# Sliding-window attention and a two-layer product: turning q and k by crossbar DMA, and storing 128 rows in one or two DMAs

## The chip, the cores and the metric

One core of one Trainium2 chip. The metric is device time in microseconds (us), the median of several executions; lower is better. Executions of one kernel mostly agree within about 1%; a run over 1.5% above the fastest of its kernel counts as slow. Ratios use the fast runs alone; medians and ranges below are of all runs. Inputs and output are float32; the kernel computes in float16 with float32 sums.

## The reference

Eight batches of 8-head attention over 576 positions (head size 64), where each position sees itself and the 127 before it, with a bias linear in the distance. The result goes token by token through two matrices with an ELU between.

```python
scores = scale * np.matmul(q, k.transpose(0, 1, 3, 2)) + bias      # bias = -slope * |distance|
attn   = softmax(where((rel >= 0) & (rel < 128), scores, -1e9))
x      = np.matmul(attn, v).transpose(0, 2, 1, 3).reshape(8 * 576, 512)
h      = x @ w_in                                                  # 512 -> 2048
g      = np.where(h > 0, h, np.exp(np.minimum(h, 0)) - 1)
out    = g @ w_out                                                 # 2048 -> 512
```

## The kernel before

One program in steps, 16 to a batch. Each step does one bank of attention scores (`sp`) and values (`av`) of the current batch, and, some steps behind, one tile of the hidden product (`hp`, 128x512) with its ELU, and four matmuls of the output (`op`). All engines run in the order in which the program lists their work, and so does SP's DMA queue. Four parts of it matter here.

q and k arrive with 4 positions per partition (`stq`). TensorE transposes ("turns") them, in four groups of eight transposes a batch, and ScalarE and VectorE copy them out of PSUM into `QK`, which keeps positions in blocks of 32 with the same remainder modulo 4:

```python
def transposes(b, hp):
    t = ps_s.tile([128, 2, 2, 4, 2, 32], F16, name="tp", tag="sps")
    ...                                        # eight nc.tensor.transpose(t[...], stq[b][...], ident)
    for odd in range(2):
        ...
        if hp % 2: nc.scalar.copy(o, i)
        else:      V.tensor_copy(o, i)
```

A finished block of attention, 128 tokens (`xn`), is turned for the hidden product. From batch 2 on (`XBAR = 2`) a crossbar DMA does it, which transposes 16-bit data while it moves them, from SP's queue:

```python
def turn(b, i):
    if b >= XBAR:
        nc.sync.dma_start_transpose(out=xT[:, :, o:o + n], in_=x[0:n, :])
        return
    ...                                        # batches 0 and 1: four TensorE transposes and a copy
```

From batch 3 on v is loaded through SP's queue too, four DMAs for 128 positions (q and k come through GpSimd's own queue). GpSimd casts v to float16, in line with the `min` that it does for each ELU:

```python
nc.sync.dma_start(t[32 * j:32 * j + 32, :, :], v[b, :, 128 * n + j:128 * n + 128:4, :]...)   # load_v
nc.gpsimd.tensor_scalar(out=VP[...], in0=vf.pop((b, n))..., ...)                                 # cast_v
nc.gpsimd.tensor_scalar(out=e, in0=e, scalar1=1.0, scalar2=0.0, op0=ALU.min, op1=ALU.max)        # hidden
```

The tokens run in blocks of 32 with the same remainder modulo 4, so a tile of 128 output rows goes back in up to four stores of 32 rows, each with a DRAM step of four rows:

```python
r.append((c - c0, out[b * S + 128 * n + p // 32:b * S + 128 * n + 128:4, :]))    # rows_of
...
for p0, rows in rows_of(512 * t + 128 * ts):
    nc.sync.dma_start(rows, ob[p0:p0 + rows.shape[0], :])                        # output
```

The softmax here doesn't subtract the row's maximum and nothing guards it: scores larger than these inputs give would overflow.

## Time and profile before

| before | value |
|---|---|
| time | 367.06 us (366.23 to 367.32, three runs) |
| span of the profiled run, clock granted to TensorE | 363.7 us, 0.995 |
| SP's queue: stores, v loads, crossbar transposes | 128 + 8 larger, 85, 30 |
| a crossbar transpose of 128x512: time in SP's queue | 1.2 us |

In the lines of the profile PE is TensorE, PEld its weight loads, DVE VectorE, ACT ScalarE, POOL GpSimd, and SPq SP's DMA queue; L451 is line 451 of the kernel.

### The profile page before, as it was taken

To read this page: it belongs to the slowest core of one execution; us is meant where nothing else is said; L and a number is where in the kernel's file an instruction comes from. 1 tells how busy PE (TensorE), PEld (TensorE's weight loads), DVE (VectorE), ACT (ScalarE), POOL (GpSimd) and SP (SyncE) were. 2 spreads that over 40 slices of the span, in tenths; PEclk is the share of its full clock that TensorE was granted. 3 is DMA by queue.
4 is the path that set the end of the run, shared out by engine and by line. 5 is a ranking of instruction groups with operands and counts; after the bars stand their busy time and mean duration, and the time that the engine had idled before them with its cause. 6 is when DMAs were issued, how large, how long until landed. Compare 5 with 4: busy or idle time off the path is not lost.

```text
span 363.7 us, 9613 instructions
## 1 busy us (share of the span) xinstructions
PE 340.3 (94%) x3790; PEld 251.6 (69%) x3790; DVE 243.5 (67%) x574; ACT 206.7 (57%) x349; POOL 145.7 (40%) x229
## 2 busy tenths in 40 slices
PE   6878997999979999989999999999999999999994
PEld 6766775777647667767777777777777777666651
DVE  6479889678886776666676767776776756634430
ACT  4355583666537655765566665666567565543431
POOL 9146623434314723472346334642433232233320
PEclk9899999999999999999999999999999999999999
DMA  8999999839243973497448934793631222211113
GB/s 114 198 206 119 228 107 183 151 80 155 38 103 89 133 108 84 110 128 110 98 94 127 127 88 100 120 136 82 102 84 45 52 47 45 51 43 47 29 43 73
DMA packets 81948, 37.06 MB, mean 102 GB/s; under 512 B 51952, under 2 KB 77296, under 8 KB 81904
## 3 DMA queue, kind: packets, MB, share of 16 engines
q0 software_dynamic: 34064, 15.40, 35.5%
q1 hardware_dynamic: 47840, 21.06, 25.6%
q8 instruction: 29, 0.48, 0.6%
q14 instruction: 15, 0.12, 0.1%
HBM read 36.70 MB, written 9.44 MB: 127 GB/s over the span
## 4 chain that ended last, share of the span: by engine, by line
PE 65%; DVE 14%; ACT 9%; DMA 7%; issue 3%; POOL 1%; SPq 0%; ACTq 0%; POOLq 0%
PE hp L451 27%; PE op L492 25%; PE sp L348 5%; ACT QK L322 5%; DVE VP L116 4%; DMA vs<-in_v_dram 3%; PE av L394 3%; DVE g L463 3%; ACT EX L372 2%; DVE QK L324 2%; ACT e L455 2%; DVE EX L380 2%; DMA xT<-xn 2%; DMA stq<-in_q_dram 1%; DVE xn L415 1%
## 5 line engine op out<-in xcount | busy, mean ns | idle before, releaser
L456 POOL TENSOR_SCALAR e<-e 128x512 f32<-128x512 f32 x144 | 88.6, 615 | 199.9 <-ACT e L455 199.9
L451 PE MATMUL hp<-xT,wi 128*128 128x256 f16 (+3 forms) x1536 | 150.3, 246 | 8.1 <-DVE g L463 3.6
L451 PEld LDWEIGHTS <-wi 128*128 128x128 f16 x1536 | 121.5, 98 | 49.9 <-DVE g L463 5.5
L455 ACT ACTIVATE e<-hp 128x512 f32<-128x512 f32 x144 | 86.0, 597 | 119.0 <-PE hp L451 110.0
L492 PE MATMUL op<-wo,g 128*128 128x512 f16 x576 | 146.4, 379 | 0.0
L463 DVE SCALAR_TENSOR_TENSOR g<-e,hp 128x512 f16<-128x512 f32 x144 | 98.0, 681 | 23.9 <-POOL e L456 22.7
L380 DVE TENSOR_TENSOR EX<-EX,band 128x512 f16<-128x512 f16 x112 | 49.8, 445 | 57.1 <-ACT EX L372 57.0
L372 ACT ACTIVATE EX<-sp 128x512 f16<-128x512 f32 x128 | 75.9, 593 | 13.3 <-PE sp L368 8.6
L492 PEld LDWEIGHTS <-g 128*128 128x128 f16 x576 | 51.2, 98 | 36.9
L348 PE MATMUL sp<-QK 128*128 128x128 f16 (+3 forms) x576 | 49.8, 213 | 0.0
L394 PE MATMUL av<-VP,EX 128*128 128x65 f16 x576 | 38.6, 193 | 4.3 <-DVE EX L380 2.7
L394 PEld LDWEIGHTS <-EX 128*128 128x128 f16 x576 | 31.6, 98 | 8.7 <-DVE EX L380 4.2
L415 DVE TENSOR_TENSOR xn<-av,rden 128x256 f16<-128x256 f32 x80 | 34.0, 424 | 2.8
L348 PEld LDWEIGHTS <-QK 128*128 128x128 f16 (+1 forms) x576 | 31.3, 97 | 1.0 <-issue 0.2
L496 ACT COPY ob<-op 128x512 f32<-128x512 f32 x36 | 21.1, 586 | 14.3 <-PE op L492 6.4
L322 ACT COPY QK<-tp 64x1024 f16<-64x1024 f16 x28 | 28.1, 1005 | 1.6 <-PE tp L312 1.4
L414 DVE RECIPROCAL rden<-av 128x4 f32<-128x4 f32 x80 | 14.4, 180 | 16.0 <-PE av L394 14.6
L134 POOL TENSOR_SCALAR VP<-vf 128x512 f16<-128x512 f32 (+1 forms) x25 | 19.5, 779 | 2.7 <-DMA vf<-in_v_dram 2.7
L324 DVE COPY QK<-tp 64x1024 f16<-64x1024 f16 x28 | 19.2, 684 | 1.1 <-PE tp L312 0.8
L312 PE MATMUL tp<-ident,stq 128*128 128x128 f16 x224 | 17.1, 219 | 2.3 <-ACT QK L322 1.0
L312 PEld LDWEIGHTS <-stq 128*128 128x128 f16 x224 | 13.8, 98 | 3.4 <-issue 3.2
L116 DVE COPY VP<-vs 32x512 f16<-32x512 f16 x48 | 14.9, 310 | 1.3 <-DMA vs<-in_v_dram 0.5
(70 smaller groups left out, 118.5 us busy)
## 6 DMA issues: line engine op xcount, KB each, us to landing
out_dram<-ob SPq DMA_DIRECT2D x128, 64.0 KB, 1.7
vf<-in_v_dram SPq DMA_DIRECT2D x80, 64.0 KB, 2.3
stq<-in_k_dram POOLq DMA_DIRECT2D x7, 512.0 KB, 6.4
stq<-in_q_dram POOLq DMA_DIRECT2D x7, 512.0 KB, 7.5
wi<-in_moe_w_in_dram POOLq DMA_DIRECT2D x4, 512.0 KB, 13.8
wo<-in_moe_w_out_dram POOLq DMA_DIRECT2D x4, 512.0 KB, 15.1
QK<-TQ SPq DMA_DIRECT2D x2, 576.0 KB, 8.0
vs<-in_v_dram POOLq DMA_DIRECT2D x2, 512.0 KB, 9.9
```

The lines of the kernel that those rows point to most:

```text
L312: nc.tensor.transpose(t[:, g, w, :, j, :], stq[b][:, w, 2 * hp + g, 2 * j:2 * j + 2, :].rearrange("p a d -> p (a d)"), ident)
L322: nc.scalar.copy(o, i)
L348: nc.tensor.matmul(t[:, o:o + n], qk[0:r, h, 1, kc:kc + 128], qk[0:r, h, 0, qc:qc + n], start=b > 0 or o == 0, stop=b > 0)
L372: nc.scalar.activation(e[:, 0:512], t, AF.Exp, scale=0.125)
L380: V.tensor_tensor(out=e, in0=e, in1=band[:, c:c + n].unsqueeze(1).broadcast_to([128, 512 // n, n]), op=ALU.min)
L394: nc.tensor.matmul(a[:, l, :], e[:, c:c + 128], vp[:, n, h, 0:D + 1], start=st, stop=sp)
L415: V.tensor_tensor(out=xnt[b, i][:, 4 * half:4 * half + 4, :], in0=a[:, :, 0:D], in1=r.unsqueeze(2).broadcast_to([128, 4, D]), op=ALU.mult)
L451: nc.tensor.matmul(p[:, l * w + u0:l * w + u1], w_in_sb[:, c, fc * 128:(fc + 1) * 128], xT[:, c, x0:x0 + u1 - u0], start=(c == 0), stop=(c ...
L455: nc.scalar.activation(e, p, AF.Exp)
L456: nc.gpsimd.tensor_scalar(out=e, in0=e, scalar1=1.0, scalar2=0.0, op0=ALU.min, op1=ALU.max)
L463: V.scalar_tensor_tensor(out=gs[t][:, f0:f0 + nf, c0:c0 + w], in0=sh(es.pop((t, j))), scalar=1.0, in1=sh(hps.pop((t, j))), op0=ALU.subtrac ...
L492: nc.tensor.matmul(ops[t], gs[t][:, fc, ts * 128:(ts + 1) * 128], w_out_sb[:, fc, :], start=(fc == 0), stop=(fc == NFC - 1))
```

## The change

Its intent: TensorE is the bound, so take the transposes of q and k of batches 2 to 7 off it (and their copies off ScalarE). The crossbar turns them, in eight DMAs a batch, and VectorE puts the result in block order, within SBUF. To make room in SP's queue, a store's rows are reordered by the DRAM side of its pattern, so that one or two DMAs do what up to four did. And the copies that place v of batch 2 move some steps earlier. The core of the diff, with cuts marked:

```diff
+        def cross(b, n):
+            w, hp = 1 - n // NP, n % NP
+            ...
+            nc.sync.dma_start_transpose(
+                out=tq[b][:, w, 2 * hp:2 * hp + 2, :, :].rearrange("p h a c -> p (h a) c"),
+                in_=stq[b][:, w, 2 * hp:2 * hp + 2, :, :].rearrange("p h j d -> p (h j d)"))
+
+        def uncross(b, n):
+            w, j = 1 - n // 4, n % 4
+            r = slice(64 * (j % 2), 64 * (j % 2) + 64)
+            V.tensor_copy(
+                QK[b % 2][0:64, :, w, 0:512].rearrange("p h (n j i) -> p h n j i", j=4, i=32)[:, :, :, j, :],
+                tq[b][r, w, :, j // 2, :].rearrange("p h (n i) -> p h n i", i=32))
...
+                n, p = divmod(o, 128)
+                k = min(128 - p, S - o, c0 + 128 - c)
+                if n < 4:
+                    rows = out[b * S + 128 * n:b * S + 128 * n + 128, :].rearrange(
+                        "(i j) d -> j i d", j=4)[p // 32:(p + k) // 32, :, :]
...
-                for hp in range(NP):
-                    at(s0 + ((5, 9, 10, 13) if b > 1 else (9, 10, 13, 14) if b else (14, 14, 15, 15))[hp],
-                       transposes, b + 1, hp)
+                if b == 0:
+                    for hp in range(NP):
+                        at((14, 14, 15, 15)[hp], transposes, b + 1, hp)
+                else:
+                    for n in range(8):
+                        at(s0 + (n if b > 1 else 6 + n // 2), cross, b + 1, n)
+                        at(s0 + (5 + n if b > 1 else 12 + n // 2), uncross, b + 1, n)
...
-        at(33, load_v4_tail, 2)
+        at(22, load_v4_tail, 2)
...
-            at(32 + n, place_v4, 2, n)
+            at(24 + 2 * n, place_v4, 2, n)
```

More of the change, by code (lines that the diff above doesn't have):

```diff
@@ L71 @@
     xT = one([128, 4, RING], F16, "xT")
-    stq, stt, vf, vs = {}, {}, {}, {}
+    stq, stt, vf, vs, tq = {}, {}, {}, {}, {}
     def load_qk(b, w, h0=0, h1=H):
@@ L324, in transposes @@
                     V.tensor_copy(o, i)
+        def cross(b, n):
+            w, hp = 1 - n // NP, n % NP
+            if n == 0:
+                tq[b] = stage.tile([128, 2, H, 2, 128], F16, name="tq", tag="tq", bufs=1)
+            nc.sync.dma_start_transpose(
[7 more added lines that the diff above has]
+                tq[b][r, w, :, j // 2, :].rearrange("p h (n i) -> p h n i", i=32))
         def transposes_tail(b):
@@ L472, in rows_of @@
                 b, o = divmod(c, S)
-                if o < 512:
-                    n, p = divmod(o, 128)
-                    r.append((c - c0, out[b * S + 128 * n + p // 32:b * S + 128 * n + 128:4, :]))
-                    c += 32
-                else:
-                    r.append((c - c0, out[c:c + 64, :]))
-                    c += 64
+                n, p = divmod(o, 128)
[3 more added lines that the diff above has]
+                        "(i j) d -> j i d", j=4)[p // 32:(p + k) // 32, :, :]
+                else:
+                    rows = out[c:c + k, :]
+                r.append((c - c0, c - c0 + k, rows))
+                c += k
             return r
@@ L496, in output @@
                 nc.scalar.copy(ob, ops[t])
-                for p0, rows in rows_of(512 * t + 128 * ts):
-                    nc.sync.dma_start(rows, ob[p0:p0 + rows.shape[0], :])
+                for p0, p1, rows in rows_of(512 * t + 128 * ts):
+                    nc.sync.dma_start(rows, ob[p0:p1, :])
         spare = ps_o.tile([128, DO], F32, name="spare", tag="op")
```

## The prediction

> **What bounds the kernel now.** I read the page's busy shares first, then the chain of work that ended last (its summary, then its pieces in order of time over one batch), then the groups of instructions for the durations of what goes, then the DMA issues and the DMA queue's timeline, because the change moves work there.
>
> The page: busy time, share of the span, and the chain's summary.
>
> ```profile
> PE 340.3 (94%) x3790; PEld 251.6 (69%) x3790; DVE 243.5 (67%) x574; ACT 206.7 (57%) x349; POOL 145.7 (40%) x229
> ...
> PE 65%; DVE 14%; ACT 9%; DMA 7%; issue 3%; POOL 1%; SPq 0%; ACTq 0%; POOLq 0%
> ```
>
> TensorE is nearly always busy and makes 65% of the chain. So removing TensorE work pays, as long as nothing else ends up in the chain. The chain in order of time shows a step of the schedule without transposes and the place where the transposes of q and k cut in:
>
> ```profile
> 205.54 0.87 PE hp L451 x8
> 206.41 0.24 PE av L394 x8
> 206.66 0.22 PE sp L348 x4
> 206.88 0.86 PE op L492 x4
> ...
> 216.08 0.87 PE hp L451 x8
> 216.95 0.12 PE av L394 x4
> 217.07 0.22 PE sp L348 x4
> 217.30 0.45 PE tp L312 x8
> 217.74 0.86 PE op L492 x4
> ```
>
> From 205.54 to 216.08 are five steps, 2.11 us each: 0.87 + 0.12 + 0.22 + 0.86 and a little more where a block begins. A group of eight transposes adds 0.45. Where ScalarE copies the result out of PSUM the chain leaves TensorE altogether:
>
> ```profile
> 199.90 1.00 ACT QK L322
> 200.90 0.01 issue
> 200.91 1.02 ACT QK L322
> 201.93 0.04 issue
> 201.97 0.39 PE tpt L330 x8
> 202.36 0.97 PE op L492 x4
> ```
>
> The same piece comes back at 239.13 and 275.90, so a batch of 16 steps takes 36.77 us. Sixteen steps at 2.11 are 33.7, with the tail's transposes (0.39, they stay) 34.1. So the transposes of q and k cost about 2.65 us a batch: 4 x 0.45 = 1.8 of TensorE, the rest waits on the copies.
>
> The groups that go, and the DMA queue's timeline of one batch start (both of before):
>
> ```profile
> L322 ACT COPY QK<-tp 64x1024 f16<-64x1024 f16 x28 | 28.1, 1005 | 1.6 <-PE tp L312 1.4
> L324 DVE COPY QK<-tp 64x1024 f16<-64x1024 f16 x28 | 19.2, 684 | 1.1 <-PE tp L312 0.8
> ```
> ```profile
> 203.98 1.73 SPq L498 DMA_DIRECT2D out_dram<-ob  x4
> 205.82 2.72 SPq L423 DMA_TRANSPOSE xT<-xn  x2
> 208.63 2.01 SPq L126 DMA_DIRECT2D vf<-in_v_dram  x4
> 212.56 2.14 SPq L498 DMA_DIRECT2D out_dram<-ob  x4
> 214.80 1.19 SPq L423 DMA_TRANSPOSE xT<-xn  x1
> 216.09 4.45 SPq L126 DMA_DIRECT2D vf<-in_v_dram  x8
> ```
>
> A crossbar transpose of 128x512 holds SP's queue for about 1.2 us (1.3 with the gap after it), a v load about 0.5, a store about 0.43. SP's queue is in order, and is free about a third of this stretch.
>
> **What the Trainium skill says.** (1) "DMA: Bandwidth & Descriptors", section "Why a DMA increments its semaphore by 16 and not by 1": a DMA runs on the largest k up to 16 that divides the slowest dimension of both access patterns, on the lowest-numbered engines. The new stores have a DRAM pattern of 4x32x512 or 2x32x512, so k would be 4 or 2 in place of 16. No run of before has such a DMA, so its trace cannot confirm it. (2) Same page, "Latency and other measured facts": a DMA transpose moves 261 GB/s; for 128 KB an estimate of 0.5 us. The trace agrees: its packet records show 32 packets of 256 B on each engine at 15 to 18 ns, 0.5 to 0.6 us, with 2.4 us from issue to landing. The crossbar itself is cheap; the issue is not. (3) "VectorE: DVE Perf Modes", "Why PSUM operands drop a tier" and the tier table before it: a copy from PSUM gets at most 2x, a 16-bit copy within SBUF 4x. The trace agrees: from PSUM 1024 elements take 684 ns and 512 take 417 (0.52 ns each); within SBUF 512 take 285 and 256 take 210 (0.29 each).
>
> **The change part by part.**
> *TensorE:* batches 2 to 7 lose 24 groups of 8 transposes, 24 x 0.45 = 10.8 us. *ScalarE* loses 24 copies of 1.005, 24 us. *VectorE* loses 24 x 0.684 = 16.4 us and gets 48 copies of 64x1024 within SBUF, estimated at 285 + 512 x 0.29 = 0.43 us each, 20.6 in all: 4 us more. It is at about 1.6 us a step, so per step (cut 0.445, elu 0.68, normalize 0.38 on average, reorder 0.43) it comes to about 2.0 with the gaps, just under TensorE's 2.11.
> *SP's queue* gets 48 transposes (48 x 1.3 = 62 us) and loses some 80 of 136 stores (about 35 us).
>
> *Batches 2 to 6 running* (they turn 3 to 7): 5 x 2.65 = 13.2 us gained at most.
>
> *Batch 1 running* (it turns batch 2): there the profile shows VectorE as the limit, the copies that place v in steps 32 to 35 (five steps from 92.27 to 107.62, 3.07 each). They move into steps 24 to 30, but the new reorders of batch 2 and both tails lie there too. VectorE over steps 24 to 31: 8 x 1.73 + 5.1 (place) + 3.7 (reorder) + 1.7 (tails) = 24.4 us against 19.1 that these steps took; steps 32 to 36 then take 5 x 2.11 = 10.6 in place of 15.3. Sum 35.0 against 34.4: nothing gained, within 2 us.
>
> *Waits for the new transposes.* I walked SP's queue over a batch start in the order of the built program, with the times above: the fourth transpose of k starts about 10 us after step 0 and lands at 11.5, when VectorE wants it at about 13; the last of q starts about 20.2 and lands 22.6, when VectorE wants it at 21.5. So VectorE waits about 1 us for q; the slack before TensorE feels it is 0.5 to 1 us (elu must end before the hidden product two steps on). After a pair of 2x32x512 stores the transposes queue on two engines behind 64 packets of 2,048 B. Such packets took 84 to 167 ns in before, median 122; with few engines writing I take the low end, 85 to 90, so 64 are 5.6 us, and then the waits are 2 to 3 us. Mean: 0.8 us a batch, 4 us in all.
>
> *A turned block that is needed soon.* Blocks of batches 2 and 3 are turned three steps before use; in before one landed late (5.5 us at 158.3, TensorE idle 1.1). Behind a pair of stores, at step 46, I expect about 2 us of new waiting.
>
> *The end.* Before, the last output copy starts at 359.1 and the last store's packets end near 362.4. The last four tiles have seven stores of 2x32x512 and one plain one. On two engines a tile needs 64 x 85 ns = 5.4 us, while TensorE finishes one every 3.45: from 347.1 they end at 352.5, 358.6, 364.0, and the last (32 packets and four of the plain store) at 367.1. That is 4.7 us later.
>
> Sum: 367.1 - 13.2 + 0.6 + 4 + 2 + 4.7 = 365.2; I lower it to 364.5, as the ScalarE time freed shortens some waits on its exps.
>
> **Rivals.** *A: the stores spread over all 16 engines after all* (if the pattern is cut otherwise). Then the end is 0.4 us shorter, the pair waits go: 367.1 - 13.2 - 0.4 + 2 = 355 to 357. For it: the stores of before with 32 or 64 rows land in 1.7 us and someone tuned this kernel. Against: the rule of (1) and the built program's pattern. One in five. *B: SP's queue becomes the bound.* For it: 27 us of issue in a batch of 34, two thirds in the first nine steps; v loads come late, so GpSimd's casts, which stand in order with its mins, hold up elu. Against: the walk above keeps up but for 1 us. It would eat all of the 13 and, with the end, give 370 to 376. One in five. *C: two-engine stores run at the median 122 ns*, 7.8 us a tile: the end grows by 12 us in place of 4.7, total 372. *D: VectorE's reorders, which read SBUF in a fast mode, slow GpSimd's mins.* The skill's "SBUF — State Buffer", section "SBUF: two separate sides", calls their port pair an exclusive lock. The mins take 615 ns, and 48 x 0.43 could be added at worst, mostly hidden since GpSimd is busy 40%: under 2 us.
>
> **Range and chances.** Step gains are read off the trace and are firm (13 us, give or take 1). What I am unsure of takes them back: the end 0 to 12, waits 0 to 12. From 356 (all but the gain small) to 374 (B or C). Faster by over 2% means under 359.7: rival A and half of the good cases of the waits, 0.30. Slower than 374.4 needs B and C together or a stall that I do not see: 0.14. Between: 0.56.
>
> **What would show it.** Right: batches 2 to 6 repeat every 34 to 36 us; no ScalarE copies of QK in the chain but for batches 0 and 1; waits of VectorE's reorder for the DMA tq<-stq of about 1 us each batch; the stores' time to landing up from 1.7 to 4 us or more; the last store landing 5 us or more after the last output copy. Wrong: stores that still land in 2 us (A); SP never waiting for a sender in the first half of a batch and VectorE or GpSimd waiting 3 us and more for DMA (B); the reorder at 0.7 us in place of 0.43.

## More of the kernel before

Start with the view of waits. A line says which engine and instruction waited, for whom, the total in us, how often, and the longest wait. Three lines of before:

```profile
PEld L451 <- DVE g L463: 5.5, 5, 1.4
...
PE hp L451 <- DVE g L463: 3.6, 6, 0.9
...
POOL VP L134 <- DMA vf<-in_v_dram: 2.7, 1, 2.7
```

TensorE hardly waits for VectorE's ELU (`g`), and GpSimd waits once for a v load. The lines on the clock and the DMA engines, in 40 equal slices of the span, in tenths:

```profile
PEclk9899999999999999999999999999999999999999
DMA  8999999839243973497448934793631222211113
```

TensorE keeps its full clock from the third slice on, and the DMA engines are about half idle after the first fifth.

## The result, and the profile after

**430.0 us** (median; 427.02 to 433.81, four runs, the last of which counts as slow) against 367.07 (366.23 to 367.32, four runs): 17% slower. The ratio is 1.169, with a 95% interval of 1.163 to 1.176. Ratios here are the mean time of one kernel's fast runs over the mean of the other's of the same rounds, so not quite the ratio of the medians quoted beside them.

The page after, the lines that answer to those of before:

```profile
PE 353.5 (83%) x3598; PEld 255.1 (60%) x3598; DVE 252.0 (59%) x598; ACT 184.9 (43%) x325; POOL 144.2 (34%) x229
...
PEclk9978999968997879869979998799996999999996
DMA  9999999992779986598898999699984435411111
...
PE 52%; DMA 25%; DVE 10%; SPq 5%; issue 2%; ACT 2%; POOL 1%; DVEq 0%; ACTq 0%; POOLq 0%
PE hp L467 23%; PE op L510 19%; DMA tq<-stq 12%; DMA xT<-xn 9%; PE sp L364 5%; PE av L410 3%; DMA vs<-in_v_dram 3%; DVE g L479 3%; DVE VP L116 2%; SPq L331 2%; SPq L439 2%; DMA stq<-in_q_dram 1%; ACT EX L388 1%; DVE EX L396 1%; DVE QK L338 1%
```

TensorE's share fell from 94% to 83%, and the chain now holds 25% of DMA and 5% of SP's queue (`SPq`): the new transposes (`tq<-stq`) 12%, the old ones (`xT<-xn`) 9%. ScalarE's copies of QK are gone from the chain, as intended. But TensorE has 192 matmuls fewer and yet is busy for 13 us longer, and its granted clock falls in many slices (mean 0.915 in place of 0.995). The waits:

```profile
DVE QK L338 <- DMA tq<-stq: 51.2, 12, 8.5
...
PE hp L467 <- DVE g L479: 41.0, 12, 7.8
...
POOL VP L134 <- DMA vf<-in_v_dram: 15.1, 7, 5.5
...
PE hp L467 <- DMA xT<-xn: 8.2, 4, 4.7
```

VectorE's reorder waits for the crossbar 51 us in all, twelve times. As VectorE is in order too, the ELU behind the reorder comes late, and TensorE waits 41 us for it: the same waits seen one engine further on. The groups:

```profile
L467 PE MATMUL hp<-xT,wi 128*128 128x256 f16 (+3 forms) x1536 | 163.6, 259 | 54.5 <-DVE g L479 41.0
...
L338 DVE COPY QK<-tq 64x1024 f16<-64x1024 f16 x48 | 23.7, 494 | 51.8 <-DMA tq<-stq 51.2
```

Now SP's queue at a batch start (start, time held, what, how many), to be laid beside the stretch of before in the prediction, and three pieces of the chain from the same stretch:

```profile
290.17 1.24 SPq L439 DMA_TRANSPOSE xT<-xn  x1
291.50 1.52 SPq L331 DMA_TRANSPOSE tq<-stq  x1
293.11 2.12 SPq L439 DMA_TRANSPOSE xT<-xn  x1
295.28 1.26 SPq L331 DMA_TRANSPOSE tq<-stq  x1
296.63 2.01 SPq L126 DMA_DIRECT2D vf<-in_v_dram  x4
298.69 1.21 SPq L331 DMA_TRANSPOSE tq<-stq  x1
300.00 0.57 SPq L516 DMA_DIRECT2D out_dram<-ob  x1
300.69 2.14 SPq L439 DMA_TRANSPOSE xT<-xn  x1
302.88 1.74 SPq L331 DMA_TRANSPOSE tq<-stq  x1
...
315.44 1.97 SPq L331 DMA_TRANSPOSE tq<-stq  x1
```
```profile
302.88 5.30 DMA tq<-stq
...
315.44 6.18 DMA tq<-stq
322.77 1.87 PE hp L467 x8
```

The queue has no gap in this stretch. The fourth crossbar transpose of q and k starts 12.7 us after the first line, the eighth 25.3 us after it, and they land 5.3 and 6.2 us after their start (the pieces of the chain run to the landing). The last piece is what follows on TensorE, at half rate. The timeline shows an earlier stall and a shorter one (start, duration, the idle time before and who ended it):

```profile
267.63 0.42 DVE L338 COPY QK<-tq 64x1024 f16<-64x1024 f16 x1 [8.54 <-DMA tq<-stq]
...
268.70 1.86 PE L467 MATMUL hp<-xT,wi 128*128 128x256 f16 x8 [7.81 <-DVE g L479]
...
309.36 1.03 PE L467 MATMUL hp<-xT,wi 128*128 128x256 f16 x8 [3.60 <-DVE g L479]
```

VectorE waits 8.54 us for the crossbar, TensorE 7.81 us for VectorE, and then runs at half rate. The Trainium skill's "TensorE: Matmul & The Clock Gate", section "What's actually happening", says that the clock falls to half after an idle window of about 3.4 us and returns after about as long a busy one. The trace agrees: eight matmuls take 1.03 to 1.04 us in this view when nothing has been amiss, still 1.03 after 3.60 us of idling, and 1.86 to 1.87 after 4.89, 5.38 and 7.81 us. (The border isn't sharp: in the run with merged transposes below 3.39 us of idling were enough.) The next ones are slow too (four of `op` at 271.00: 1.91 us in place of 1.03), so a long wait costs its own length and some 2 us more.

Where is the time lost? Each batch has one spot that is easy to find, VectorE's copy of the tail's transposes in step 14 (`QK<-tpt`). Its start in each batch, from the timelines:

| start of that copy in batch, us | 1 | 2 | 3 | 4 | 5 | 6 | end of span |
|---|---|---|---|---|---|---|---|
| before | 89.2 | 129.1 | 166.4 | 203.4 | 240.2 | 277.0 | 363.7 |
| after | 98.6 | 151.4 | 198.7 | 242.9 | 288.7 | 334.2 | 427.9 |
| later by | 9.4 | 22.3 | 32.2 | 39.5 | 48.5 | 57.2 | 64.2 |

Every batch that turns q and k by crossbar loses 7 to 13 us, and the end another 7. (Of batch 1's 9.4 us, 2.6 were lost by step 25 of the program, 1.7 of them at the start.)

### The profile page after: what moved, and what is told of

Same layout as the page of the kernel before. It is cut to its first block, busy times and chain, and to the rows that moved or that the text cites. A ratio compares the mean times of both kernels' runs of the same rounds, so it can differ in the third digit from the quotient of the medians.

```text
span 427.9 us, 9192 instructions
## 1 busy us (share of the span) xinstructions
PE 353.5 (83%) x3598; PEld 255.1 (60%) x3598; DVE 252.0 (59%) x598; ACT 184.9 (43%) x325; POOL 144.2 (34%) x229
## 4 chain that ended last, share of the span: by engine, by line
PE 52%; DMA 25%; DVE 10%; SPq 5%; issue 2%; ACT 2%; POOL 1%; DVEq 0%; ACTq 0%; POOLq 0%
PE hp L467 23%; PE op L510 19%; DMA tq<-stq 12%; DMA xT<-xn 9%; PE sp L364 5%; PE av L410 3%; DMA vs<-in_v_dram 3%; DVE g L479 3%; DVE VP L116 2%; SPq L331 2%; SPq L439 2%; DMA stq<-in_q_dram 1%; ACT EX L388 1%; DVE EX L396 1%; DVE QK L338 1%
## 5 line engine op out<-in xcount | busy, mean ns | idle before, releaser
L467 PE MATMUL hp<-xT,wi 128*128 128x256 f16 (+3 forms) x1536 | 163.6, 259 | 54.5 <-DVE g L479 41.0
L467 PEld LDWEIGHTS <-wi 128*128 128x128 f16 x1536 | 130.4, 104 | 102.7 <-issue 57.5
L510 PE MATMUL op<-wo,g 128*128 128x512 f16 x576 | 153.7, 394 | 0.0
L338 DVE COPY QK<-tq 64x1024 f16<-64x1024 f16 x48 | 23.7, 494 | 51.8 <-DMA tq<-stq 51.2
L364 PE MATMUL sp<-QK 128*128 128x128 f16 (+3 forms) x576 | 52.1, 220 | 0.9 <-DVE QK L338 0.5
L410 PE MATMUL av<-VP,EX 128*128 128x65 f16 x576 | 40.3, 198 | 4.2 <-DVE EX L396 2.5
L364 PEld LDWEIGHTS <-QK 128*128 128x128 f16 (+1 forms) x576 | 33.0, 101 | 2.1 <-issue 0.6
L430 DVE RECIPROCAL rden<-av 128x4 f32<-128x4 f32 x80 | 14.2, 178 | 22.1 <-PE av L410 21.1
L523 PE MATMUL spare<-ident 128*128 128x128 f16 x94 | 9.0, 272 | 1.6 <-DVE ident L175 1.6
L523 PEld LDWEIGHTS <-ident 128*128 128x128 f16 x94 | 8.1, 126 | 1.7 <-DVE ident L175 1.6
L352 DVE COPY QK<-tpt 64x512 f16<-64x512 f16 x16 | 6.7, 418 | 0.2
## 6 DMA issues: line engine op xcount, KB each, us to landing
wi<-in_moe_w_in_dram POOLq DMA_DIRECT2D x4, 512.0 KB, 10.8
```

Of the source, the lines that this page charges most:

```text
L338: V.tensor_copy(QK[b % 2][0:64, :, w, 0:512].rearrange("p h (n j i) -> p h n j i", j=4, i=32)[:, :, :, j, :], tq[b][r, w, :, j // 2, :].re ...
L364: nc.tensor.matmul(t[:, o:o + n], qk[0:r, h, 1, kc:kc + 128], qk[0:r, h, 0, qc:qc + n], start=b > 0 or o == 0, stop=b > 0)
L410: nc.tensor.matmul(a[:, l, :], e[:, c:c + 128], vp[:, n, h, 0:D + 1], start=st, stop=sp)
L467: nc.tensor.matmul(p[:, l * w + u0:l * w + u1], w_in_sb[:, c, fc * 128:(fc + 1) * 128], xT[:, c, x0:x0 + u1 - u0], start=(c == 0), stop=(c ...
L510: nc.tensor.matmul(ops[t], gs[t][:, fc, ts * 128:(ts + 1) * 128], w_out_sb[:, fc, :], start=(fc == 0), stop=(fc == NFC - 1))
```

## The experiments

Theory at the outset (S): the stores that run on few DMA engines hold the transposes up. Rival (T): SP's queue has too much to issue, whatever the stores. The runs were made in four lots, each beside runs of the kernel before (367.6 to 368.6 us, median of the lot). Fourteen kernels ran, all with correct results.

**First the rule on which theory S rests**: how many engines does a store use? In the packet records of SP's queue each DMA closes with 4-byte packets, one for each engine that it uses, a transpose with 32. Before: 226 plain DMAs of 16 and 30 transposes of 32 make 4,576; counted: 4,576. After: 78 transposes x 32 + 98 plain ones x 16 + 16 stores (4x32x512) x 4 + 32 stores (2x32x512) x 2 = 4,192; counted: 4,192. (The same sums come out in the runs with merged transposes, 4,960, and with the new stores and no transpose, 1,696.) So the new stores do run on four and two engines, as the prediction took from the skill. Its rival A is out.

**Old stores, the rest of the change** (one part undone).

```diff
-                for p0, p1, rows in rows_of(512 * t + 128 * ts):      # and rows_of as before
-                    nc.sync.dma_start(rows, ob[p0:p1, :])
+                for p0, rows in rows_of(512 * t + 128 * ts):
+                    nc.sync.dma_start(rows, ob[p0:p0 + rows.shape[0], :])
```

> The changed kernel with the stores of before (four DMAs of 32 rows, each over 16 engines), all else as changed. Theory S (the few-engine stores are the cause: 64 packets on each of two or four engines stand ahead of every later DMA of SP's queue, and a transpose that waits on one engine holds its packets open on all): 355 to 365 us, tq and xT landing in 2.5 to 4 us again, no packets of over 2 us. Theory T (48 more crossbar transposes are too much, whatever the stores: SP's issue, or transposes holding each other up): 410 us or more, VectorE still waiting some 40 us for tq.

Measured: 410.76 us, ratio 1.117 (1.110 to 1.123). So the transposes alone cost 42 us and the stores 19 of the 63. Its profile: slow (416.99 us, clock 0.937), so I take from it only what the waits are for:

```profile
DVE QK L338 <- DMA tq<-stq: 55.1, 12, 10.7
PE hp L467 <- DVE g L479: 53.7, 16, 10.1
```

The crossbar's data land within a median of 2.7 us of their issue here, yet VectorE waits as long as in the changed kernel. So few-engine stores aren't needed for the waits, and the time is in T's range. Late issue isn't all of it, though: in the two longest waits of this run (10.7 and 9.5 us) VectorE had waited for 3.6 and 2.7 us when the transpose was issued, which then took 7.0 and 6.8 us to land. The run with unread transposes, a fast one, shows what they met.

**The new stores alone, in the kernel before** (the reverse edit in the other kernel).

> The kernel before with the new stores alone (two or four engines). Theory S: its 30 transposes of xn get caught too, and the end is 6 us longer: 373 to 385 us, with packets of some us around the turns. Theory T: the end alone, 371 to 374 us.

Measured: 388.19 us, ratio 1.051 (1.044 to 1.059): the stores cost 20 us without any new transpose, more than either theory said. The chain and SP's queue at the worst place:

```profile
210.41 15.86 DMA xT<-xn
```
```profile
209.17 1.13 SPq L500 DMA_DIRECT2D out_dram<-ob  x2
210.41 4.06 SPq L423 DMA_TRANSPOSE xT<-xn  x1
```

A crossbar transpose behind a pair of two-engine stores holds the queue for 4.06 us in place of 1.2 and lands 15.9 us after its start. (Loads of k and q by GpSimd's queue, issued at 208.26 and 212.98, run in this stretch too.) The waits for turned blocks:

```profile
PE hp L451 <- DMA xT<-xn: 10.3, 3, 4.3
PEld L451 <- DMA xT<-xn: 9.0, 2, 4.8
```

By the copy of step 14, batches 1 to 6 are 2.8, 6.7, 13.7, 14.9, 16.7 and 16.7 us later than before. The first 2.8 us are there in step 12 of batch 0 already, before any store, so they aren't the stores'. The loss comes mostly in batches 2 and 3 (their blocks are turned three steps before use) and then at the end (24 us later there).

**Rows reordered on chip, so that a store of 64 rows uses 16 engines** (the changed kernel with fewer stores that spread).

```diff
-                            p[:, l * w + u0:l * w + u1], w_in_sb[:, c, fc * 128:(fc + 1) * 128],
-                            xT[:, c, x0:x0 + u1 - u0], ...)
+                            p[:, l * w + u0:l * w + u1].rearrange("p (g i j) -> p g j i", i=32, j=2),
+                            w_in_sb[:, c, fc * 128:(fc + 1) * 128],
+                            xT[:, c, x0:x0 + u1 - u0].rearrange("p (g j i) -> p g j i", i=32, j=2), ...)
...
+                        "(i j) d -> i j d", j=4)[:, p // 32:p // 32 + 2, :]        # the store's DRAM side
```

> The changed kernel, with rows put in order when the hidden product is written to PSUM, so that each 64 rows are one store whose DRAM pattern is 32x2x512, which divides over 16 engines: as few stores as changed, but on all engines. Theory S: 353 to 363 us, a little under e1 since SP issues 72 stores and not 136. Theory T: 410 or more. If the strided PSUM write slows TensorE, hp matmuls get longer than 258 ns at full clock.

Measured: 466.0 us, ratio 1.269, a miss, though useful. Hidden matmuls that write PSUM with a step of two elements take 364 ns each in place of 246 to 259 (TensorE 96% busy, clock 0.996). VectorE waits for the crossbar only 4.3 us here: with steps that long, SP's queue keeps up. The edit adds a cost of its own, so it can't be read as a trial of the stores.

**Stores issued by ScalarE** (old stores; `nc.sync.dma_start` becomes `nc.scalar.dma_start` for them).

> As e1, but the 16-engine stores are issued by ScalarE's queue, so SP's queue has 136 issues less. Theory S: 352 to 363 us; if SP's issue was what made transposes late, faster than e1 by 3 us or more, else the same. Theory T by SP's issue: well under 430, 380 to 400. Theory T by transposes holding each other: 410 or more.

Measured: 416.36 us, ratio 1.131 (1.123 to 1.138); its profile is slow. The waits for the crossbar fall to 5.2 us, as they should if SP's queue was too full, but ScalarE, in order like the others, now carries the stores' issue (10% of the chain) and waits that the profile puts down to stores (28.6 us before its exps). One in-order queue is relieved, another loaded. By its time alone the run fell to the branch "transposes holding each other" (410 or more); the short waits for the crossbar speak against that reading, but ScalarE's load keeps the run from deciding.

**The reorders three steps later** (old stores), to see if slack is all that is missing.

```diff
-                        at(s0 + (5 + n if b > 1 else 12 + n // 2), uncross, b + 1, n)
+                        at(s0 + (8 + n if b > 1 else 12 + n // 2), uncross, b + 1, n)
```

> As e1 (changed kernel, 16-engine stores of before), but VectorE's reorders for batches 3 to 7 stand three steps later (steps 8 to 15 of the batch before, not 5 to 12). Theory Q (SP's in-order queue falls behind its schedule, VectorE stands at the reorder until the transpose lands, TensorE then idles and comes back at half clock): the waits go, 360 to 372 us, VectorE's wait for tq under 12 us in place of 55. Theory R (transposes are slow in themselves or slow other DMAs, whenever they are used): 395 us or more.

Measured: 405.53 us, ratio 1.102 (1.095 to 1.110): a miss, and by its time on the side of theory R. The waits:

```profile
POOL VP L134 <- DMA vf<-in_v_dram: 49.5, 11, 8.6
...
DVE QK L338 <- DMA tq<-stq: 15.9, 5, 4.4
```

VectorE's waits fall from 55 to 16 us, and GpSimd's waits for v rise from 7 to 50. The v loads stand behind the transposes in the same queue; GpSimd's casts wait for them, its mins stand behind the casts, and the ELU behind the mins. So the lateness belongs to the queue and not to one consumer. Theory R (transposes slow in themselves) is left to the merged run below.

**The same with the new stores.**

> The changed kernel with its few-engine stores, and the reorders three steps later as in e5. Theory Q with the stores as a second cause of their own (e2 showed 20 us): 378 to 395 us, some 15 to 20 over e5. If the stores act only by delaying the transposes, the slack hides them and it is within 7 us of e5 (the end).

Measured: 431.66 us, ratio 1.172 (1.163 to 1.181). It is 26 us above the run before, with 60.3 us of waits for v and 18.4 for turned blocks: the stores cost no less when the reorders have slack.

**Transposes that nobody reads** (the kernel before, its q and k turned by TensorE as ever, with the 48 crossbar transposes added into a tile without a reader).

```diff
...
+                if b:
+                    for n in range(8):
+                        at(s0 + (n if b > 1 else 6 + n // 2), cross, b + 1, n)
```

> The kernel before, everything kept, plus the 48 transposes of the change issued where the change issues them, into a tile that nobody reads. Nobody waits for them, so what they cost is what they do to the others of SP's queue (v, xT, stores) and to the DMA engines. Theory Q: v and xT come late, GpSimd waits some 30 to 50 us for v: 385 to 405 us. If only VectorE's own wait for tq mattered: 367 to 371.

Measured: 398.23 us, ratio 1.083 (1.079 to 1.088): 31 us for transposes whose data land in a median of 2.5 us and are wanted by no one. The largest wait for a DMA, in all, and its longest case (the load of k, the piece of the chain, the cast):

```profile
POOL VP L134 <- DMA vf<-in_v_dram: 45.9, 10, 9.1
```
```profile
208.50 0.94 POOL L80 DMA_DIRECT2D stq<-in_k_dram  x1
...
212.81 6.40 DMA vf<-in_v_dram
...
219.38 0.62 POOL L134 TENSOR_SCALAR VP<-vf 128x512 f16<-128x512 f32 x1 [9.06 <-DMA vf<-in_v_dram]
```

This shows that more transposes in SP's queue cost time by making the rest of the queue late, without anyone waiting for them. How the lateness grows is seen in the longest case. The last DMA of v was issued 2.5 us after GpSimd's wait had begun, and then landed after 6.40 us in place of the median 2.5: it stood behind a load of k. The packet records have a stretch of 1.15 us (212.24 to 213.39) with 396 packets of that load and not one of SP's queue. In before the last v load is issued at 227.53 and the k load at 230.14, with nothing of v landing late there. The other two waits of about 7 us here, the four longest of the run with late reorders, and the two longest with old stores follow a k load in the same way. No run moved the k load, so how much of the 31 us it makes stays open.

**Eight transposes merged into two** (old stores). The same bytes, in two DMAs of 128x2048 a batch.

```diff
             nc.sync.dma_start_transpose(
-                out=tq[b][:, w, 2 * hp:2 * hp + 2, :, :].rearrange("p h a c -> p (h a) c"),
-                in_=stq[b][:, w, 2 * hp:2 * hp + 2, :, :].rearrange("p h j d -> p (h j d)"))
+                out=tq[b][:, w, :, :, :].rearrange("p h a c -> p (h a) c"),
+                in_=stq[b][:, w, :, :, :].rearrange("p h j d -> p (h j d)"))
...
-                        at(s0 + (n if b > 1 else 6 + n // 2), cross, b + 1, n)
+                        if n % NP == 0:
+                            at(s0 + (n // 2 if b > 1 else 6 + n // 2), cross, b + 1, n)
```

> As e1, with the reorders where the change has them, but the eight transposes of a batch are two of 16 blocks each. If SP pays per DMA (1.2 us whatever its size), its queue has 7.8 us less a batch, and theory Q gives 365 to 385 us; if it pays per block of 128x128, the issue of one takes 4 to 5 us and the time stays at 405 to 415. Theory R: 400 or more either way.

Measured: 373.52 us, ratio 1.015 (1.008 to 1.022): of the 42 us, 37 are gone. No reorder waits for the crossbar any more. SP's queue, two merged transposes and a single one of a turned block:

```profile
254.97 1.71 SPq L331 DMA_TRANSPOSE tq<-stq  x1
...
260.84 3.04 SPq L331 DMA_TRANSPOSE tq<-stq  x1
...
266.01 1.19 SPq L439 DMA_TRANSPOSE xT<-xn  x1
```

The twelve merged transposes hold the queue for 1.7 to 6.4 us each (median 2.4), 33.8 us in all, where the 48 singles of the run before held it for 67.5. The same bytes cost half the queue's time, so much of the cost goes with the number of DMAs, and theory R is out.

**The same with the new stores.**

> As e7 (two transposes of 16 blocks a batch), but with the changed kernel's few-engine stores. If the stores are a cause of their own, as e2 against before (20 us), e1 against the change (19) and e6 against e5 (26) say: 390 to 400 us. If with short issue the queue has room for their long landing: within 8 us of e7, the end alone.

Measured: 412.0 us, ratio 1.120 (1.115 to 1.124), so the few-engine stores cost 38 us on top of the merged transposes, more than on top of nothing (20) and more than expected. GpSimd waits 27.7 us for v (10.2 at once) and TensorE 14.0 for turned blocks.

**Do the stores cost by themselves, or by what stands behind them?** Two kernels without any crossbar transpose (the kernel before with `XBAR = 8`, so all attention blocks are turned on TensorE), one with the new stores and one with the old.

> The kernel before with no crossbar transpose at all (batches 2 to 7 turn their attention blocks on TensorE and copy them with VectorE, as batches 0 and 1 do), with the new stores on few engines. It is to be read against the run after it, which differs in the stores alone. Theory H (a few-engine store costs mainly by holding transposes up that stand behind it): with no transpose left the new stores cost only their longer end, 5 to 8 us over the old stores. Theory I (they cost by themselves, slowing v loads and everything else): 15 us and more over the old stores.

> As the run before it, with the old stores. TensorE gains 30 groups of four transposes (about 0.25 us each, 7 to 8 us) and VectorE 30 copies: 370 to 378 under either theory. Its difference to the run before decides between H (5 to 8 us) and I (15 us and more).

Measured: 379.71 us (ratio 1.034, 1.030 to 1.038) with the new and 372.78 us (1.014, 1.009 to 1.018) with the old: 6.9 us apart. In batches 2 to 6 the copy of step 14 starts within 0.25 us of the other's (283.42 against 283.65 in batch 6; in batch 1 it is 1.5 us, made up by batch 2). The last output copies start together too, and then one ends 11.7 us later, the other 5.0:

```profile
367.10 0.59 ACT L498 COPY ob<-op 128x512 f32<-128x512 f32 x1 [2.87 <-PE op L494]
```
```profile
367.34 0.58 ACT L496 COPY ob<-op 128x512 f32<-128x512 f32 x1 [2.87 <-DMA out_dram<-ob]
```

(new stores first; spans 378.8 and 372.3.) So without crossbar transposes behind them few-engine stores cost nothing in the middle of this kernel, and 6.7 us at the end. That the transposes behind them make the rest in the other kernels follows by comparison with the 20 us above; what in the DMA engines makes a transpose wait so long behind such a store isn't settled by these runs.

**The third part alone**: the earlier placing of batch 2's v in the kernel before.

> The kernel before with the third part of the change alone: v of batch 2 placed in steps 24 to 30 and its tail loaded at step 22. By VectorE's budget in the prediction (18.4 + 5.1 us in steps 24 to 31, then 10.6) the same within 3 us: 363 to 369. Neither theory needs it to differ; a loss of 5 us or more would be a cause of its own.

Measured: 366.18 us, ratio 0.996 (0.989 to 1.003): neutral.

**Can the expected gain be had?** Old stores, merged transposes (for batches 4 to 7 issued two steps earlier), and the crossbar for batches 3 to 7 alone (batch 2 stays on TensorE).

```diff
-                if b == 0:
+                if b <= 1:
                     for hp in range(NP):
-                        at((14, 14, 15, 15)[hp], transposes, b + 1, hp)
+                        at(s0 + ((9, 10, 13, 14) if b else (14, 14, 15, 15))[hp], transposes, b + 1, hp)
                 else:
                     for n in range(8):
-                        if n % NP == 0:
-                            at(s0 + (n // 2 if b > 1 else 6 + n // 2), cross, b + 1, n)
-                        at(s0 + (5 + n if b > 1 else 12 + n // 2), uncross, b + 1, n)
+                        if not n & 3:
+                            at((s0 - 2 + n // 2 if b > 2 else s0 + n // 2), cross, b + 1, n)
+                        at(s0 + 5 + n, uncross, b + 1, n)
```

> The candidate for a version better than both: 16-engine stores of before, batch 2 still turned by TensorE, batches 3 to 7 by two transposes each of 16 blocks, issued for batches 4 to 7 at steps -2 and 0 where SP's queue is empty; v of batch 2 placed as changed. Theory Q (SP's issue time is what counts): 354 to 362 us, VectorE and GpSimd waiting under 5 us for tq and v. Theory R (crossbar traffic itself is the trouble): no better than e7's 373.

Measured: 366.9 us, ratio 0.999 (0.994 to 1.004): no gain, and above the expected 354 to 362. But batches 4, 5 and 6 now follow each other in 35.5, 35.2 and 34.9 us (the copies of step 14: 173.51, 208.97, 244.14, 279.05) in place of 36.8 to 37.0. The gain of those batches is eaten in batch 3, where a turned block comes late and the clock falls:

```profile
161.63 8.17 DMA xT<-xn
169.93 1.87 PE hp L467 x8
```

This trace also shows what a reorder costs: alone 0.42 us, but 0.83 us where it begins during one of GpSimd's casts:

```profile
190.03 0.83 DVE L338 COPY QK<-tq 64x1024 f16<-64x1024 f16 x1
...
192.37 0.42 DVE L338 COPY QK<-tq 64x1024 f16<-64x1024 f16 x1
```
```profile
189.80 0.79 POOL L134 TENSOR_SCALAR VP<-vf 128x512 f16<-128x512 f32 x1
```

The Trainium skill's "SBUF — State Buffer", section "SBUF: two separate sides", has VectorE and GpSimd share a pair of ports under an exclusive lock that whoever starts first keeps for a whole instruction. The trace agrees: all twelve reorders that begin during a cast end 0.27 to 0.28 us after the cast does (190.86 against 190.59 here), where 0.42 us alone would have ended before it. The cast's 0.79 us, in place of 0.62 alone, is not the reorder's doing: in before, without reorders, 24 of the 25 casts take 0.78 to 0.79 too, each begun while VectorE was at work on `EX`.

**The crossbar for batches 5 to 7 alone**, to stay clear of the tight blocks.

```diff
-                if b <= 1:
+                if b <= 3:
                     for hp in range(NP):
-                        at(s0 + ((9, 10, 13, 14) if b else (14, 14, 15, 15))[hp], transposes, b + 1, hp)
+                        at(s0 + ((5, 9, 10, 13) if b > 1 else (9, 10, 13, 14) if b else (14, 14, 15, 15))[hp], transposes, b + 1, hp)
```

> The version of the ninth run (old stores, two merged crossbar transposes a batch), but with the crossbar for batches 5 to 7 alone; batches 3 and 4 stay on TensorE, where the blocks of attention are still turned three steps before their use and one came 5.8 us late. Theory: the crossbar gains 1.7 us a batch (35.0 to 35.1 in place of 36.77) where nothing waits for it, so 3 x 1.7 = 5 us: 361 to 363, and no wait of a hidden product for its turned block above 3 us. Rival: the v loads and stores behind the merged transposes hold up GpSimd's casts in these batches too, and the time is that of before, 365 to 368.

Measured: 364.79 us, ratio 0.9935 (0.9885 to 0.9985), five rounds. It is the only version whose interval lies ahead of the kernel before, by 0.65%, or 2.4 us of the 5 expected. Its profile, slow (436 us), says nothing on where the rest went; that stays open.

## Why the prediction was wrong

It said 364.5 us (356 to 374); the kernel takes 430.0. By its own steps:

- *The gain on TensorE* (13.2 us at most for batches 2 to 6): right in kind, about two thirds of the size. With the queue relieved, batches follow in 34.9 to 35.5 us in place of 36.8 to 37.0, so 1.5 to 1.9 us less and not 2.65. It never shows in the changed kernel.
- *Waits for the new transposes*, "0.8 us a batch, 4 us in all": **this is the step that failed.** The walk of SP's queue said that the fourth transpose starts about 10 us into the batch and lands within 1.5 us, the last starts at 20.2 and lands 2.4 us later. Counted from the turn at the batch start the trace has 12.7 and 25.3 us, with landings after 5.3 and 6.2. The reorders waited 51.2 us in all. The walk began from a misread line: the queue is said to be free for about a third of the stretch shown, but its lines hold it for 14.2 of 16.6 us, so a seventh was free; a third holds for the whole batch (23.6 of 36.8 us held), and the new transposes go where the queue was fullest. Then three costs were too small or left out. A transpose held the queue for 1.63 us (`tq`) and 1.95 us (`xT`) on average in the changed kernel, not 1.2 to 1.3. Landings of 5 us and more, behind few-engine stores or behind the loads of k and q, weren't in it. And whatever else stood in the queue (v loads, turned blocks) was late with it. The slack before TensorE feels a wait, 0.5 to 1 us, was right: VectorE's 8.54 us came through as 7.81. Rival B named this mechanism, SP's queue as the bound with GpSimd's casts and mins behind it, and was the right one, but mis-sized: it counted on 370 to 376, that is the loss of the gain, and not on a queue that delays every batch by 7 to 13 us.
- *Stores that hold up transposes* were in the sum with 2 us for turned blocks, and for some pairs inside the 4 us of the step before. By the runs they cost 19 to 20 us, of which the end is 6.7; so about 12 to 13 where a few were put. The packets themselves were as fast as assumed (84 to 96 ns for most of those of 2,048 bytes, against 85 to 90), so rival C is out. The largest delay, 15.9 us from start to landing, is about three times the 5.6 us that the prediction allowed a pair of stores.
- *The clock* wasn't in the prediction at all. TensorE should have been busy for 340.3 - 10.8 = 329.5 us and was for 353.5, 24 us more. The groups have it: with as many matmuls as before, `hp` took 163.6 us in place of 150.3, `op` 153.7 in place of 146.4, and the scores and values 4 us more. These 24 us of busy time are part of the 63, and the slow matmuls stand behind the long waits.
- *The end*, 4.7 us later: right in kind, 2 us short. It is 6.7 (from the start of the last output copy to the end of the span 11.3 us in place of 4.6). The sum's four tiles also slip: 352.5 + 5.4 is 357.9, not 358.6.
- *Batch 1 unchanged within 2 us*: wrong in the changed kernel, where it ends 9.4 us late, 6.8 of them after step 25, by the same waits. The placing of v by itself was indeed neutral.
- *A reorder of 0.43 us*: right alone (0.42); the mean is 0.494, as 12 of the 48 begin during a GpSimd instruction and take up to double (rival D, small as foreseen). *Rival A* is refuted by the packet count.

The sum of causes: about 42 us from the transposes in SP's queue (after with old stores, less before), about 19 from the stores, of these 6.7 at the end. The two overlap differently in other company (20, 19, 26 and 38 us for the stores in four pairs of runs with transposes behind them, 7 in the one without), so the split is good to some us only. Not separated are the loads of k and q in GpSimd's queue, which the late transposes and v loads meet.

## What to carry to other kernels

Count a DMA queue's issue time like an engine's busy time, and walk it with what stands *behind* the new work: a queue, VectorE and GpSimd are each in order, so the first late item delays consumers that have nothing to do with it, and a DMA that is late enough meets traffic of other queues that it used to miss. Fewer DMAs, each larger, do the same bytes for less (eight transposes into two: 37 of 42 us back), but cutting the number of stores by a pattern that leaves them two or four engines can cost more than the issue it saves, above all with crossbar transposes behind it. And when TensorE may wait over 3 us at a time, add the half-rate matmuls that follow.

## What the Trainium skill lacked or had wrong

- "DMA: Bandwidth & Descriptors", section "Issuing engines are not separate DMA queues", calls the time to initiate a DMA usually small relative to the DMA itself. Not so for the crossbar here: a 128x512 transpose holds SP's queue for 1.19 us (`xT` in before) to 1.26 us (`tq` with the unread transposes) in the median, twice the 0.5 to 0.6 us that its packets take and half of the 2.4 us to its landing. Four times the size holds it for 1.7 to 6.4 us (median 2.4). The page has cycle counts for some transposes of earlier generations, none for four or sixteen blocks within SBUF.
- The same page's rule on the number of engines, section "Why a DMA increments its semaphore by 16 and not by 1", holds (4,192 closing packets counted as worked out). It lacks the consequence: a crossbar transpose behind a two-engine store held the queue for 4.06 us and landed after 15.9 us (with loads of k and q on the way), while the kernel without transposes lost no time to plain loads behind such stores (copies of step 14 within 0.25 us of each other from batch 2 on).
- The same page has no figure for what a load from GpSimd's queue does to SP's: behind a 512 KB load of k, v landed after 6.4 us in place of 2.5.
- A matmul that writes PSUM with a step of two elements takes 364 ns in place of 246 to 259. "Advanced Engine Details and Errata" has a warning on such patterns, in its section "PSUM Cachelines", but no figure.
